# The second pass of a token mix: the 64 leftover rows ahead of the first pair of row tiles

## The chip, the cores and the metric

The kernel runs on one core of one Trainium2 chip. Its time is device microseconds of one execution; the figure for the kernel before is the median of three runs. The profile is of one execution, and its times are counted from the span's start.

## The reference

Two stages follow each other. The first is a long convolution of x (8 batches, 5696 steps, 128 channels) with h along the steps, by an FFT. The second takes its result as x:

```python
theta = x @ w_theta
zr, zi = x * np.cos(theta), x * np.sin(theta)
y = np.einsum('ts,bsd->btd', w_tok_r, zr) + np.einsum('ts,bsd->btd', w_tok_i, zi)
u = x + y
out = u + np.maximum(u @ w_ch, 0.0)
```

The token mix, two 5696 x 5696 matrices against 5696 x 1024 values, is most of the matmul work, and the only part that the change touches.

## The kernel before

**The mix in two passes.** The 5696 steps are two halves of 2816 and 64 leftover ones. The contraction over s runs in two passes p, one for each half of s; the leftover s (`zl`) are added in the second pass. The output rows are 22 tiles of 128 in each half and 64 leftover rows. One step of the loop is a pair tt: tile tt of the first half together with tile 22 + tt of the second, for both halves of the batch, four sums of 128 x 512. Pass 0 leaves its sums in `cp_hbm`, pass 1 reads them as addends (`addend`), adds its own and hands each finished 128 x 512 tile to an output stage (`u_stage`: a transpose on TensorE, a copy on ScalarE, a product with `w_ch`, the maximum and sum on VectorE, a store).

**Stretches.** Each pair runs over 11 b tiles j (a b tile holds 128 contraction rows: real and imaginary parts of 64 steps, 4 blocks of 512 columns), in stretches of 3, 3, 3 and 2. `prepare(i)` makes the weights of stretch i: W is loaded as it lies in memory by GpSimd's queue into a ring of six slots (`load_w`, L504), and `w_t` (L709) transposes it on VectorE, one instruction of 128 x 384 words for each of the four blocks of W.

**Seven products or eight.** Most pairs use Strassen's scheme: seven products per j and r (L1079) instead of eight, into seven accumulators M1 to M7 in the order M3, M4, M5, M2, M1, M7, M6. It needs sums of W (`w_sum`, L718) and sums of b (`sum_ops`, L650: three into new blocks of the b tile, M3, M4 and M1, and two in place, over M6 and M7). A few pairs (`plain`) take the eight products of the plain scheme (L1000), which needs b as it was loaded: in pass 1 that is pair 0, so that the b sums can be made while it runs. The leftover rows (`tt is None`, L943 to L983) are 64 rows: 4 products per j and r (L963, L965) of 64 columns of weights, which still stream 512 columns of b. They take W from the matrices' last 64 rows, in loads of half the size.

**The start of pass 1.** `pairs` (L450) sets the order: in pass 1 pair 0, then the leftover, then pairs 1 to 21. `start_pass` (L834) issues, on ScalarE's DMA queue, the loads of the 11 b tiles of the second half (two of 512 KB each, L634), which wait until pass 0 has read the tiles; and on SyncE the two loads of `zl`, whose sum is made on VectorE (L842). While pair 0's stretches run, the first two b sums of each tile are issued (L1058); in the leftover, the other three (L971). The leftover uses W sums (`sa`, L864) with M2, M3, M4 and M5, and the accumulators of M1 and M7.

**The order of the instructions.** Each engine works through its own list. A scheduler orders them, but for VectorE between (1, 0, 0) and (1, 1, 0), i.e. from pass 1's pair 0 to its pair 1, where the order is as written (`manual_schedule`, L911). At the end of a pair that is followed by another pair (`woven`), the transposes for the next pair are put between the evacuations of the accumulators; ahead of the leftover they are made before the last stretch's matmuls. The output stages of a pair wait in a list (`spread`) and are issued one per stretch by `aside` (L935): the first half after one product, the second after another; in the leftover around its matmuls (L950, L968). DMAs on the hardware queues (SyncE's and ScalarE's) share eight semaphores, and each waits for the landing of the one before it on its own.

Of the kernel before, what the change touches and what calls it, by code (L numbers as in the profile page):

```python
# [22 lines left out]
def kernel(  # L23
# [423 lines left out]
                    nc.sync.dma_start(z_hbm[r, p_, j, q_, i], z[rows])  # L447

    CHUNKS = [(j0, min(CJ, NJ - j0)) for j0 in range(0, NJ, CJ)]
    pairs = (list(range(21)) + [None, 21], [0, None] + list(range(1, 22)))  # L450
    chunks = [(p, tt, c) for p in range(2) for tt in pairs[p] for c in range(len(CHUNKS))]
    ring = {"n": 0, "read": set(), "wl": 0, "upto": 0}
    loaded = {}
# [194 lines left out]
    def sum_ops(bt):  # L648
        b11, b12, b21, b22 = (bt[q] for q in (M2, M6, M7, M5))
        return [lambda f=f, x=x: f(*x) for f, x in (  # L650
            (nc.vector.tensor_sub, (bt[M3], b12, b22)), (nc.vector.tensor_sub, (bt[M4], b21, b11)),
            (nc.vector.tensor_add, (bt[M1], b11, b22)), (nc.vector.tensor_add, (b12, b11, b12)),
            (nc.vector.tensor_add, (b21, b21, b22)))]
# [53 lines left out]
    def w_t(wb, j0, nj, ng=4, pool=None):  # L707
        wt = (pool or tp).tile([P, TJ, P, 2], BF16, tag="ws" if pool else "wt", name="wt")
        nc.vector.transpose(  # L709
            wt.rearrange("p j t r -> p (j t r)").bitcast(F32).rearrange(  # L710
                "p (j g t) -> p g j t", j=TJ, g=4)[:, :ng, :nj],
            wb[:, :ng, j0 * 64:(j0 + nj) * 64].bitcast(F32).rearrange(
                "p g (j s) -> p g j s", j=nj))
        return wt

    def w_sum(x0, x1, op, nj, m=P):
        out_ = sp.tile([P, TJ, P, 2], BF16, tag="ws")
        nc.vector.tensor_tensor(out_[:, :nj, :m], x0[:, :nj, :m], x1[:, :nj, :m], op=op)  # L718
        return out_
# [88 lines left out]
    def addend(p, k, ti, h, m=P):  # L808

        tag = f"c{k}"  # L810
        if p == 1:
            tag = ("c0", "c1", "c2", "c3", "red", "mag")[tags["n"] % 6]
            tags["n"] += 1
        c = cp.tile([P, 512], F32, tag=tag, name=f"c{k}")
        if p == 0 and ti in (22, 23):
            yT = cp.tile([P, 4, P], BF16, tag=f"yy{k}", name=f"yy{k}")
            nc.sync.dma_start(yT, yt_hbm[:, 4 * h:4 * h + 4, ti * P:ti * P + P])
            return c, yT
        if p == 0:
            yy = cp.tile([P, 512], BF16, tag=f"yy{k}", name=f"yy{k}")  # L820
            nc.sync.dma_start(yy[:m], half(y2_hbm, ti, h)[:m])
            return c, yy
        nc.sync.dma_start(c[:m], half(cp_hbm, ti, h)[:m])
        return c, c
# [26 lines left out]
    def prepare(i, at_once=True):  # L851
        if i >= len(stretches):
            return None
        k, p, tt, j0, s0, nj = stretches[i]
        pump()

        def read():
            if s0 + nj == CHUNKS[chunks[k][2]][1]:
                ring["read"].add(k)
                pump()  # L860
        if tt is None:
            a1, a2 = (w_t(loaded[k][n], s0, nj, ng=2) for n in range(2))
            read()
            return a1, a2, w_sum(a1, a2, add, nj, m=64)  # L864
        w11, w12, w21, w22 = (loaded[k][n] for n in range(4))
        if plain(p, tt):
            a = {}

            def some(n):
                if n in (0, 1):  # L870
                    a[n] = w_t((w11, w12)[n], s0, nj)
                elif n in (4, 5):
                    a[n - 2] = w_t((w21, w22)[n - 4], s0, nj, pool=sp)
            if not at_once and p:
                return a, some
            for n in range(6):
                some(n)
            read()
            return a if at_once else (a, lambda n: None)
        a = {}  # L880

        def step(n):

            if n == 0:
                a[M3] = w_t(w11, s0, nj)
            elif n == 1:
                a[M4] = w_t(w22, s0, nj)
            elif n == 2:
                a["12"] = w_t(w12, s0, nj)
                a[M5] = w_sum(a[M3], a["12"], add, nj)  # L890
            elif n == 3:
                a["21"] = w_t(w21, s0, nj)
                a[M2] = w_sum(a["21"], a[M4], add, nj)
            elif n == 4:
                a[M1] = w_sum(a[M3], a[M4], add, nj)
            elif n == 5:
                a[M7] = w_sum(a["12"], a[M4], ALU.subtract, nj)
            else:
                a[M6] = w_sum(a["21"], a[M3], ALU.subtract, nj)
        if at_once:  # L900
            for n in range(7):
                step(n)
            read()
            return a
        return a, step
# [1 line left out]
    nxt, second, st = None, None, {}  # L907
    ordered = ExitStack()
    for i, (k, p, tt, j0, s0, nj) in enumerate(stretches):
        if (p, tt, j0 + s0) in ((0, 0, 0), (1, 0, 0)):  # L910
            ordered.enter_context(tc.manual_schedule(engines={mybir.EngineType.DVE}))  # L911
        elif (p, tt, j0 + s0) in ((0, 2, 6), (1, 1, 0)):
            ordered.close()
# [18 lines left out]
        a, nxt = nxt, None if i == 1 else prepare(i + 1, not woven)  # L932
        if woven:
            nxt, step = nxt
        def aside(first_of, second_of):  # L935
            nonlocal second
            if first_of and spread and (p == 1 or (tt > 0 and not end_of_pair)):
                where_bg["tags"] = ("c2", "c3") if j0 + s0 == TJ else ("red", "mag")
                _, first, second = spread.pop(0)
                with tc.issue_after(sides["late"].ins) if p == 0 and tt == 1 else ExitStack():  # L940
                    first()
                    if len(spread) > 1:
                        spread[1][0]()  # L943
            if second_of and second is not None:
                second()
                second = None

        if tt is None:
            if p:
                aside(True, False)  # L950
            if first_of_pair:
                ps = [mps.tile([P, 512], F32, tag=f"m{q}", name=f"m{q}") for q in ((M1, M7) if p else (M3, M4))]
                cs = [addend(p, h, NT - 1, h, m=64) for h in range(2)]
            a1, a2, sa = a
            terms = ((sa, M2, a2, M4), (a1, M3, sa, M5))
            for j in range(nj):
                jj = j0 + s0 + j
                for r in range(2):
                    b = [x[:, r, :] for x in bts[jj]]
                    st_ = jj == 0 and r == 0  # L960
                    sp_ = jj == NJ - 1 and r == 1 and zl is None
                    for h, (x0, q0, x1, q1) in enumerate(terms):
                        nc.tensor.matmul(ps[h][:64], x0[:, j, :64, r], b[q0],  # L963
                                         start=st_, stop=False)
                        nc.tensor.matmul(ps[h][:64], x1[:, j, :64, r], b[q1],  # L965
                                         start=False, stop=sp_)
            if p:
                aside(False, True)  # L968
            if p == 1:
                for j in range(nj):  # L970
                    for op in sum_ops(bts[j0 + s0 + j])[2:]:  # L971
                        op()
            if end_of_pair:
                if zl is not None:
                    wl = wl_room()
                    nc.sync.dma_start(wl[:, :64], wl_hbm[:, NT - 1, :64])
                    for h in range(2):
                        nc.tensor.matmul(ps[h][:64], wl[:, :64], zl[h], start=False, stop=True)
                for h in range(2):
                    c, c0 = cs[h]  # L980
                    nc.vector.tensor_add(c[:64], c0[:64], ps[h][:64])
                    finish(p, NT - 1, h, c, m=64)
            continue  # L983
        classic = plain(p, tt)
        if first_of_pair and i:
            ms = [mps.tile([P, 512], F32, tag=f"m{q}", name=f"m{q}") for q in (range(7) if not classic else (M3, M4, M5, M2) if p else (M2, M6, M1, M7))]
        if first_of_pair:
            where = ((tt, 1), (22 + tt, 0), (tt, 0), (22 + tt, 1))
            if zl is not None:
# [3 lines left out]
        if j0 + s0 == (3 if classic else 2) * TJ:  # L993
            cs = (sides["cs"] if p == 0 and tt == 0 else
                  [addend(p, n, t, h) for n, (t, h) in enumerate(where)])

        def product(a, jj, j, n, hs):
            for r in range(2):
# [30 lines left out]
        if classic:  # L1029
# [24 lines left out]
            for j in range(nj):  # L1054
                if p == 0:
                    done["used"] = tt * (j0 + s0 + nj)
                else:
                    for op in sum_ops(bts[j0 + s0 + j])[:2]:  # L1058
                        op()
        else:  # L1060
            left = {}
# [80 lines left out]
```

## Time and profile before

| | |
|---|---|
| median of three runs | 2114.66 us (2113.42 to 2116.9) |
| the profiled execution | 2114.66 us, span 2112.9 us |
| TensorE (PE) busy | 2000.1 us, 95% of the span |
| VectorE (DVE) busy | 1593.8 us, 75% |
| mean of one 128 x 512 x 128 matmul (L1079), pipelined | 380 ns |
| one b sum, 128 x 1024 (L650) | 649 to 685 ns |
| DMA share of 16 engines, 1260 to 1314 us | full |

The busy time of a matmul is from its start to its modelled end, and the next starts before that; so starts are compared, not busy times. "Idle before, releaser" behind a row of the timeline says how long the engine did nothing ahead of it and what ended that. The chain of waits goes back from the last instruction to what released it, step by step. The granted clock is the share of its full clock that TensorE had.

### The profile page before, as it was taken

To read this page: it belongs to the slowest core of one execution; us is meant where nothing else is said; L and a number is where in the kernel's file an instruction comes from. 1 tells how busy PE (TensorE), PEld (TensorE's weight loads), DVE (VectorE), ACT (ScalarE), POOL (GpSimd) and SP (SyncE) were. 2 spreads that over 40 slices of the span, in tenths; PEclk is the share of its full clock that TensorE was granted. 3 is DMA by queue.
4 is the path that set the end of the run, shared out by engine and by line. 5 is a ranking of instruction groups with operands and counts; after the bars stand their busy time and mean duration, and the time that the engine had idled before them with its cause. 6 is when DMAs were issued, how large, how long until landed. Compare 5 with 4: busy or idle time off the path is not lost.

```text
span 2112.9 us, 41491 instructions
## 1 busy us (share of the span) xinstructions
PE 2000.1 (95%) x15765; PEld 1115.9 (53%) x15765; DVE 1593.8 (75%) x2884; ACT 674.1 (32%) x997; POOL 906.6 (43%) x1662
## 2 busy tenths in 40 slices
PE   4788889878999999999999999999999999999998
PEld 3787888754444444444444444444444444444444
DVE  7767767776878888888886756877777777776867
ACT  5877878874332333232310000111111111111111
POOL 5301010237444636354556544445454444545450
PEclk8698889999999999999999999999999999999999
DMA  7357474999989989898999879768788887879793
GB/s 144 96 130 168 114 183 108 237 251 242 179 152 179 178 172 168 170 177 173 176 163 156 141 145 293 127 113 153 135 145 143 138 150 129 155 128 155 126 155 89
DMA packets 408264, 334.95 MB, mean 159 GB/s; under 512 B 85927, under 2 KB 358439, under 8 KB 407079
## 3 DMA queue, kind: packets, MB, share of 16 engines
q0 software_dynamic: 225952, 156.72, 52.4%
q1 hardware_dynamic: 176128, 164.05, 27.1%
q10 hardware_dynamic: 5984, 11.54, 1.6%
q8 instruction: 123, 2.02, 0.4%
q14 instruction: 77, 0.63, 0.1%
HBM read 377.11 MB, written 92.49 MB: 222 GB/s over the span
## 4 chain that ended last, share of the span: by engine, by line
PE 67%; DVE 3%; DMA 1%; issue 1%; POOL 0%; ACT 0%; DVEq 0%
PE m L1079 61%; PE m L1000 2%; DVE b L650 1%; PE v L796 1%; PE utp L789 1%; PE m L1083 1%; DVE c L1086 1%; DVE wt L709 1%; PE m L963 0%; PE m L965 0%; PE tpz L737 0%; PE theta_ps L391 0%; POOL ring L504 0%; DMA ring<-in_moe_w_tok_r_dram 0%; DMA wl<-in_moe_w_tok_i_dram 0%
## 5 line engine op out<-in xcount | busy, mean ns | idle before, releaser
L504 POOL DMA_DIRECT2D ring<-in_moe_w_tok_i_dram x720 | 387.9, 546 | 659.6 <-DVE wt L709 587.7
L709 DVE STREAM_TRANSPOSE wt<-ring 128x384 f32<-128x384 f32 (+2 forms) x720 | 358.6, 522 | 121.7 <-PE m L1079 70.6
L504 POOL DMA_DIRECT2D ring<-in_moe_w_tok_r_dram x720 | 386.4, 546 | 148.6 <-DVE wt L709 88.3
L1079 PE MATMUL m<-b,wt 128*128 128x512 bf16 x1640 | 389.2, 380 | 2.0 <-DVE wt L709 1.7
L1079 PEld LDWEIGHTS <-wt 128*128 128x128 bf16 x1804 | 176.5, 98 | 218.8 <-DVE wt L709 6.5
L1086 DVE TENSOR_TENSOR c<-c,m 128x512 f32<-128x512 f32 x412 | 264.7, 667 | 0.4 <-PE m L1079 0.4
L791 ACT ACTIVATE ring<-utp 128x512 bf16<-128x512 bf16 (+1 forms) x86 | 50.9, 592 | 586.7 <-PE utp L789 586.7
L323 PE MATMUL ps<-r_u,u_t 128*128 128x128 f16 x1024 | 130.8, 227 | 7.0 <-DVE u_t L307 6.3
L324 PE MATMUL ps<-r_v,v_t 128*128 128x128 f16 x1024 | 129.9, 227 | 0.0
L786 ACT ACTIVATE ub<-c 128x512 bf16<-128x512 f32 (+1 forms) x90 | 56.3, 628 | 213.2 <-DMA ring<-in_moe_w_tok_r_dram 120.9
L1000 PE MATMUL m<-b,wt 128*128 128x512 bf16 x480 | 112.5, 385 | 7.5 <-DMA b<-z_hbm 3.9
L129 POOL DMA_DIRECT2D x<-in_x_dram x64 | 33.9, 535 | 193.6 <-PE ps L193 181.1
L323 PEld LDWEIGHTS <-u_t 128*128 128x128 f16 x1024 | 105.7, 103 | 8.1 <-DVE u_t L307 8.1
L324 PEld LDWEIGHTS <-v_t 128*128 128x128 f16 x1024 | 104.8, 102 | 3.0 <-DVE v_t L307 1.3
L305 ACT ACTIVATE xs<-ps 128x1024 f16<-128x1024 f32 x96 | 95.3, 1017 | 13.2 <-DVE v_t L307 7.9
L307 DVE TENSOR_TENSOR u_t<-xs,hs 128x1024 f16<-128x1024 f16 x96 | 69.8, 727 | 33.4 <-ACT xs L305 23.6
L193 PE MATMUL ps<-f_t,x 89*128 89x180 f16 x512 | 82.0, 315 | 8.7 <-ACT xs L305 6.7
L1000 PEld LDWEIGHTS <-wt 128*128 128x128 bf16 x528 | 51.2, 99 | 68.9 <-issue 8.1
L211 PEld LDWEIGHTS <-w_t 64*128 64x128 f16 x3240 | 61.0, 102 | 36.5 <-issue 23.4
L193 PEld LDWEIGHTS <-x 89*128 89x128 f16 x512 | 73.4, 233 | 11.0 <-issue 10.1
L393 ACT ACTIVATE red<-theta_ps,magic 128x512 f32<-128x512 f32 (+1 forms) x46 | 31.6, 687 | 134.6 <-PE theta_ps L391 107.8
L739 ACT ACTIVATE ring<-tpz 128x512 bf16<-128x512 bf16 (+1 forms) x46 | 27.5, 597 | 131.7 <-PE tpz L737 111.0
(2912 smaller groups left out, 3883.3 us busy)
## 6 DMA issues: line engine op xcount, KB each, us to landing
ring<-in_moe_w_tok_r_dram POOLq DMA_DIRECT2D x352, 96.0 KB, 4.5
ring<-in_moe_w_tok_i_dram POOLq DMA_DIRECT2D x352, 96.0 KB, 4.8
ring<-in_moe_w_tok_r_dram POOLq DMA_DIRECT2D x352, 80.0 KB, 4.4
ring<-in_moe_w_tok_i_dram POOLq DMA_DIRECT2D x352, 80.0 KB, 3.9
hs<-hf_hbm SPq DMA_DIRECT2D x192, 128.0 KB, 3.3
cp_hbm<-c SPq DMA_DIRECT2D x88, 256.0 KB, 2.2
c<-cp_hbm SPq DMA_DIRECT2D x88, 256.0 KB, 4.5
out_dram<-c SPq DMA_DIRECT2D x88, 256.0 KB, 4.2
```

The source lines that it names most:

```text
L193: nc.tensor.matmul(ps[:, i // 2, (i % 2) * 2 * K1:(i % 2 + 1) * 2 * K1], lhs(q + i), f1_t[:NB], start=True, stop=True)
L211: nc.tensor.matmul(ps[:, e, j * HD:(j + 1) * HD], w_t2[rows, c0 + j, N2 * (1 - ri):N2 * (3 - ri)], a_st["a"][rows, ri * K1 + c0 + j, :], s ...
L305: nc.scalar.activation(xs[:, :, :, :ck], ps, AF.Copy)
L307: nc.vector.tensor_tensor(uv[r][:, :, :, c0:c0 + ck], xs[:, :, :, :ck], hv[:, r:r + 1, :, :ck].to_broadcast([P, 2, HD, ck]), op=mult)
L323: nc.tensor.matmul(o, u_t[:, at:at + P], r_u, start=True, stop=False)
L324: nc.tensor.matmul(o, v_t[:, at:at + P], r_v, start=False, stop=True)
L504: nc.gpsimd.dma_start(wb[32 * i:32 * i + 32, :ng, :nj * 64], bass.AP(tensor=a.tensor, offset=a.offset + row0 * S + p * H + i * QR + j0 * 6 ...
L709: nc.vector.transpose(wt.rearrange("p j t r -> p (j t r)").bitcast(F32).rearrange("p (j g t) -> p g j t", j=TJ, g=4)[:, :ng, :nj], wb[:, : ...
L786: nc.scalar.activation(ub[:m].rearrange("p b d -> p (b d)"), c[:m], AF.Copy)
L1000: nc.tensor.matmul(ms[n // 2 * 2 + h], a[n][:, j, :, r], bts_of[p][jj][n % 2 * 2 + h][:, r, :], start=(n % 2 == 0 and jj == 0 and r == 0), ...
L1079: nc.tensor.matmul(ms[q], a[q][:, j, :, r], bts[jj][q][:, r, :], start=(jj == 0 and r == 0), stop=(jj == NJ - 1 and r == 1 and q not in left))
L1086: nc.vector.tensor_tensor(c, z, ms[q], op=op)
```

## The change

In pass 1 the order becomes leftover, pair 0, pairs 1 to 21. With it:

- the leftover uses no W sums: its two sums are a1 x M2 + a2 x M7 and a1 x M6 + a2 x M5, with b as loaded, in the accumulators of M2 and M6; pair 0 takes those of M7, M5, M1 and M3 (it had M3, M4, M5, M2);
- three b sums of each tile (M3, M4, M1) are issued in the leftover, the two in place in pair 0;
- no output stage is issued in the leftover; pair 0's four come in pair 1, and the leftover's two in pair 0;
- pair 0's transposes aren't woven into the last stretch of pass 0 any more (the stretch before the leftover makes its transposes at once);
- VectorE's written order begins with the leftover.

```diff
-    pairs = (list(range(21)) + [None, 21], [0, None] + list(range(1, 22)))
+    pairs = (list(range(21)) + [None, 21], [None] + list(range(22)))
...
-            return a1, a2, w_sum(a1, a2, add, nj, m=64)
+            return a1, a2, None if p else w_sum(a1, a2, add, nj, m=64)
...
         if plain(p, tt):
-            a = {}
-
-            def some(n):
-                if n in (0, 1):
-                    a[n] = w_t((w11, w12)[n], s0, nj)
-                elif n in (4, 5):
-                    a[n - 2] = w_t((w21, w22)[n - 4], s0, nj, pool=sp)
-            if not at_once and p:
-                return a, some
-            for n in range(6):
-                some(n)
+            a = [w_t(w11, s0, nj), w_t(w12, s0, nj), w_t(w21, s0, nj, pool=sp), w_t(w22, s0, nj, pool=sp)]
             read()
             return a if at_once else (a, lambda n: None)
...
-        if (p, tt, j0 + s0) in ((0, 0, 0), (1, 0, 0)):
+        if (p, tt, j0 + s0) in ((0, 0, 0), (1, None, 0)):
             ordered.enter_context(tc.manual_schedule(engines={mybir.EngineType.DVE}))
...
         if tt is None:
-            if p:
-                aside(True, False)
             if first_of_pair:
-                ps = [mps.tile([P, 512], F32, tag=f"m{q}", name=f"m{q}") for q in ((M1, M7) if p else (M3, M4))]
+                ps = [mps.tile([P, 512], F32, tag=f"m{q}", name=f"m{q}") for q in ((M2, M6) if p else (M3, M4))]
...
-            terms = ((sa, M2, a2, M4), (a1, M3, sa, M5))
+            terms = (((a1, M2, a2, M7), (a1, M6, a2, M5)) if sa is None else
+                     ((sa, M2, a2, M4), (a1, M3, sa, M5)))
...
-            if p:
-                aside(False, True)
             if p == 1:
                 for j in range(nj):
-                    for op in sum_ops(bts[j0 + s0 + j])[2:]:
+                    for op in sum_ops(bts[j0 + s0 + j])[:3]:
                         op()
...
-            ms = [... for q in (range(7) if not classic else (M3, M4, M5, M2) if p else (M2, M6, M1, M7))]
+            ms = [... for q in (range(7) if not classic else (M7, M5, M1, M3) if p else (M2, M6, M1, M7))]
...
                 else:
-                    for op in sum_ops(bts[j0 + s0 + j])[:2]:
+                    for op in sum_ops(bts[j0 + s0 + j])[3:]:
                         op()
```

As built, VectorE has four instructions less (the leftover's W sums of pass 1), and PE, ScalarE, GpSimd and SyncE have as many as before in another order. On PE the leftover's first stretch is ordered by accumulator: twelve matmuls into M2, then twelve into M6. At the end of pair 0 the list of PE is: pair 0's last matmuls, the transposes and then the product of an output stage, then pair 1's first matmuls. On VectorE: pair 0's four evacuations, then three transposes for pair 1. On SyncE the leftover's two addends are loaded behind `zl` and the stores of pass 0's last pair, and two of pair 0's four addends far ahead of them, during pass 0. On GpSimd the leftover's four W loads stand ahead of pair 0's eight.

More of the change, by code (lines that the diff above doesn't have):

```diff
@@ L934 @@
             nxt, step = nxt
[L935 to L946, printed above, removed]
         if tt is None:
-            if p:
-                aside(True, False)
             if first_of_pair:
-                ps = [mps.tile([P, 512], F32, tag=f"m{q}", name=f"m{q}") for q in ((M1, M7) if p else (M3, M4))]
+                ps = [mps.tile([P, 512], F32, tag=f"m{q}", name=f"m{q}") for q in ((M2, M6) if p else (M3, M4))]
                 cs = [addend(p, h, NT - 1, h, m=64) for h in range(2)]
             a1, a2, sa = a
-            terms = ((sa, M2, a2, M4), (a1, M3, sa, M5))
+            terms = (((a1, M2, a2, M7), (a1, M6, a2, M5)) if sa is None else
+                     ((sa, M2, a2, M4), (a1, M3, sa, M5)))
             for j in range(nj):
@@ L985 @@
         if first_of_pair and i:
-            ms = [mps.tile([P, 512], F32, tag=f"m{q}", name=f"m{q}") for q in (range(7) if not classic else (M3, M4, M5, M2) if p else (M2, M6, M1, M7))]
+            ms = [mps.tile([P, 512], F32, tag=f"m{q}", name=f"m{q}") for q in (range(7) if not classic else (M7, M5, M1, M3) if p else (M2, M6, M1, M7))]
         if first_of_pair:
@@ L995, with aside @@
                   [addend(p, n, t, h) for n, (t, h) in enumerate(where)])
+        def aside(first_of, second_of):
+            nonlocal second
+            if first_of and spread and (p == 1 or (tt > 0 and not end_of_pair)):
+                where_bg["tags"] = ("c2", "c3") if j0 + s0 == TJ else ("red", "mag")
+                _, first, second = spread.pop(0)
+                with tc.issue_after(sides["late"].ins) if p == 0 and tt == 1 else ExitStack():
+                    first()
+                    if len(spread) > 1:
+                        spread[1][0]()
+            if second_of and second is not None:
+                second()
+                second = None
         def product(a, jj, j, n, hs):
```

## The prediction

> **What bounds the kernel now.** I read the page's busy row and chain first, for the whole span.
>
> ```profile
> PE 2000.1 (95%) x15765; PEld 1115.9 (53%) x15765; DVE 1593.8 (75%) x2884; ACT 674.1 (32%) x997; POOL 906.6 (43%) x1662
> ...
> PE 67%; DVE 3%; DMA 1%; issue 1%; POOL 0%; ACT 0%; DVEq 0%
> ```
>
> TensorE (PE) sets the end; only a few per cent of the chain are waits. The change touches the start of the second pass alone, and leaves the number of matmuls as it is. So the question is how many microseconds PE loses there, before and after. The timeline of PE gives the stage's ends:
>
> ```profile
> 1283.08 1.03 PE L1000 MATMUL m<-ring,wt 128*128 128x512 bf16 x4
> ...
> 1346.04 0.62 PE L978 MATMUL m<-zl,ring 128*64 128x512 bf16 x2
> 1348.40 1.03 PE L1079 MATMUL m<-ring,wt 128*128 128x512 bf16 x2 [1.75 <-DVE wt L709]
> ...
> 1386.18 0.59 PE L1079 MATMUL m<-ring,wt 128*128 128x512 bf16 x2
> ```
>
> Pair 0 starts at 1283.08, the leftover ends at 1346.66, pair 1 starts at 1348.40, pair 2 at 1386.18: 103.1 us. Matmuls of 512 columns start 0.2158 us apart (pair 2's next stretch of 6 in 1.295 us). Pair 0 has 180, the leftover 90, pair 1 158: 428 x 0.2158 = 92.4. A full output stage costs PE 0.45 (pair 2 takes 1422.07 - 1386.18 = 35.89, less 158 x 0.2158, over four), a 64-row one about 0.4: four and two give 2.6. Pure work: **95.0 us; lost now: 8.1 us.** Where, the chain of waits says:
>
> ```profile
> 1335.70 5.41 DVE b L650 x9
> ...
> 1342.96 4.89 DVE b L650 x8
> 1347.86 0.50 DVE wt L709
> 1348.40 5.76 PE m L1079 x18
> ```
>
> VectorE (DVE) is late: nine sums of the leftover's stretch stand ahead of the transposes that PE waits for. Behind the 1.75 us of idle the clock is at half for one stretch of 3.4 us from 1348.5 (granted clock 0.96 over 1348 to 1386, 1.00 around it). Why DVE is late is in its own timeline, and in the DMA view of 1257 to 1316:
>
> ```profile
> 1291.15 0.42 DVE L842 TENSOR_TENSOR zl<-zl,zl 128x512 bf16<-128x512 bf16 x1 [4.47 <-DMA zl<-zl_hbm]
> ...
> 1303.34 0.58 DVE L709 STREAM_TRANSPOSE wt<-ring 128x384 f32<-128x384 f32 x1 [5.37 <-DMA ring<-in_moe_w_tok_r_dram]
> 1309.41 0.58 DVE L709 STREAM_TRANSPOSE wt<-ring 128x384 f32<-128x384 f32 x1 [5.50 <-DMA ring<-in_moe_w_tok_i_dram]
> ```
> ```profile
> q10 hardware_dynamic: 5984, 11.54, 55.6%
> q0 software_dynamic: 6204, 3.82, 43.7%
> q1 hardware_dynamic: 1510, 2.47, 12.8%
> ```
>
> The 22 half tiles of b (11.54 MB), the W loads and the small transfers fill all 16 DMA engines for 59 us; DVE idles 10.9 us for W. This case's b is just in time: b10's first half, issued at 1302.52, lands at 1313.82; pair 0 needs it at about 1315.
>
> **The change, part by part.**
>
> *The leftover first, pair 0 second.* PE's counts stay: 90 and 180. But PE eats the b tiles twice as fast: 24 matmuls per stretch of three tiles (5.2 us) instead of 48 (10.4). Without any wait the leftover would run from 1283.1 to 1302.5, and would need b10 from 1300.4, 15 us sooner than now. This is the term that decides.
>
> When does the last b half land? The three queues' shares give 32.8, 25.8 and 7.6 us of full DMA time, 66.2 in 59, so I scale by 0.89: 2.54 us per MB of b, 6.0 of W, 2.74 of the small ones. b needs 29.3 us whatever happens. Of W, the leftover's loads (48 and 40 KB each instead of 96 and 80) now come ahead of pair 0's, and six ring slots gate the rest: the first pair's end 0.6 MB, the leftover 0.70, two loads of pair 0 0.77, two more (freed by the transposes of the leftover's second stretch, near 1289) 0.77, a part of the next two 0.16: 3.0 MB, 18.1 us, against 23.0 now. Small transfers 6. Sum 53.4: b lands by 1310.4; I take **1310**. Bounds: at the bare 2.54 us per MB, if W yields wholly, PE isn't held by b (1257 + 29.3 = 1286); with nothing gained, 1316, the present end of the full stretch. The middle is nearest to the row because W keeps a load in flight most of the time.
>
> With b10 at 1310, eight matmuls and the two of zl follow (2.2): the leftover ends at 1312.2 instead of 1302.5. **Loss 9.7 us.** It covers DVE's own chain: zl lands near 1288 to 1291 (its second half is issued when b4's second half lands, 1285.16 now, on the same DMA semaphore), the second stretch's transposes are queued behind that add, then three times nine sums (5.5 each by the rows above) with two half transposes (0.63 a pair) between, then pair 0's transposes: 1289 + 0.6 + 16.5 + 1.3 = 1307.4 to 1310, sooner than 1312.2. So DVE is hidden, but only by some 2 to 5 us; if b came early, DVE would be the bound.
>
> *Four sums of W less (L718), half transposes sooner.* 3 x 0.36 + 0.29 = 1.4 us of DVE, not on the path. Nothing. The leftover's loads and transposes stand in the same number; pair 0's second half of W comes later but pair 0 needs it 20 us after its start.
>
> *M2 and M6 for the leftover.* M6 is the accumulator that pass 0 empties last (1286.03 to 1286.68). The changed program puts twelve matmuls into M2 first, from M2's own evacuation at about 1283.4, so M6 is asked for at 1286.0: 0.3 us, within the 9.7.
>
> *b sums split 3 and 2 instead of 2 and 3.* 55 sums of 0.61 as before. The two in place now stand in pair 0 (10.4 us of PE for 3.7 of DVE) instead of three in the leftover (5.2 for 5.5): that removes the present wait for late sums, the **8.1 us** above with its half clock.
>
> *Pair 0 directly ahead of pair 1.* Pair 1's first transposes were made ahead of the leftover's end; now they stand on DVE behind pair 0's last two evacuations. After PE's last matmul: about 0.2 to the result, 1.28 for two evacuations (1321.92, L1041), 0.5 for a transpose, 0.1: 2.1 us. On PE an output stage is queued there too (its four transposes, then a wait for ScalarE's copy, 0.60, then four matmuls); it lies within the gap and fills 0.45 of it. **Net 1.7.** Behind it are pair 1's matmuls alone. The idle is like the 1.75 us that brought the half clock: 3.4 us at half, **1.7** more. Bounds 0 and 3.4 (a second such stretch in the leftover's stalls).
>
> The Trainium skill, TensorE: Matmul & The Clock Gate, "Why this matters for your kernels", asks for no idle gap over some 3 us; by it this gap would leave the clock alone and the result would be 1.7 lower. This trace has the half clock behind a gap of 1.75.
>
> *Output stages moved from the leftover to pair 1, ScalarE's and SyncE's orders with them.* Same count; two leftover ones go to pair 0, four to pair 1, whose reserve is that of pair 2 (35.89 with four). On SyncE zl keeps its place; two addends of pair 0 go far ahead, two of the leftover behind the first two stores. Nothing.
>
> **Sum.** 95.0 + 9.7 + 1.7 + 1.7 = 108.1 against 103.1: +5.0. The profiled execution took 2114.66 (span 2112.9 and 1.8 around it), which is also the median of the runs. **2114.66 + 5.0 = 2119.7 us.**
>
> **Rivals.**
>
> *b keeps its pace.* ACT's and POOL's queues both always have work, and halved W loads only follow each other sooner; b10 lands at 1316. For it: b's halves land 2.4 us apart whatever W load is beside them. Against it: the ring has no free slot around 1285. Leftover end 1318.2, loss 15.7, a second half clock 1.7: 95.0 + 15.7 + 3.4 + 1.7 = 115.8, +12.7: 2127.4. DMA: Bandwidth & Descriptors of the Trainium skill, "Queues, rings and completion order", has the engines take turns between queues packet by packet, which speaks for this one: b's share then does not depend on how large a W load is. No run here shows it yet.
>
> *A tie.* b lands at 1306 to 1307, when DVE is ready too: loss 6, gap 1.7, half clock 1.7: 104.4, +1.3: 2116.
>
> *Faster: DVE's late sums were the only cost.* With W out of the way (the ring is empty from about 1285 to 1289) b10 lands before 1303.5; then DVE's chain alone, with zl at 1287, starts pair 0 at 1306, loss 3.5, gap 1.7, no half clock: 100.2, -2.9: 2111.8; with zl before PE's need as well, down to 2109. It decides from b10 at 1303.5; for it the 10.9 us of DVE idle on W that go, against it the 53 us of DMA work.
>
> That the change does nothing is excluded: the built program's order shows the leftover's 90 matmuls ahead of pair 0's.
>
> **How the numbers follow.** Forecast (2118 to 2123) 0.43; b keeps its pace 0.15; tie 0.22; faster 0.20, of which 0.13 ends over 0.2% below. 0.2% (4.2 us) is about what a measurement of this kernel tells from no change; the forecast lies just over it. Slower 0.43 + 0.15 = 0.58; same 0.22 + 0.07 = 0.29; faster 0.13. The range takes in the rivals' centres: 2111 to 2128.
>
> **What would show it.** Right: the leftover starts at 1283, its fourth stretch waits on "DMA b" and it ends near 1312; the sums' share of the chain falls; a gap of 2 us ahead of pair 1 that ends with a transpose, with a granted clock under 1.00 behind it; pair 2 starts near 1391. Wrong: no wait on b (then DVE's sums must be the releaser and the time is below before's), or waits on W ahead of pair 0, which I cost at nothing; or b10 landing past 1313.

## The result and the profile after

| | before | after |
|---|---|---|
| median of four runs each | 2114.28 us (2113.42 to 2116.9) | **2124.3 us** (2121.02 to 2128.6) |
| the profiled execution | 2114.66 us, span 2112.9 | 2124.24 us, span 2122.5 |
| pass 1's first matmul to pair 2's first | 103.1 us | 112.2 us |

The change makes the kernel slower: 1.0046 times the time before, 95% interval [1.0026, 1.0067]. The forecast was 2119.7, with 2111 to 2128 as its range. The two profiled executions differ by 9.6 us, and the stage between pass 1's start and pair 2 alone by 9.1. The rest of the program is as long as it was within 0.5 us, so the loss is in the stage that the prediction looked at. (In the changed kernel pair 0's products are L989, the leftover's L941 and L943, those of the pairs behind L1068; numbers below L860 are as before.)

The page's busy row and the shares of the chain show little, as TensorE still sets the end with the same work. Of the chain, DVE has 1% where it had 3, and DMA 2% where it had 1, and that is the story in short:

```profile
PE 1998.5 (94%) x15765; PEld 1115.6 (53%) x15765; DVE 1596.1 (75%) x2880; ACT 676.1 (32%) x997; POOL 908.0 (43%) x1662
...
PE 67%; DMA 2%; DVE 1%; issue 1%; POOL 0%; ACT 0%; DVEq 0%; ACTq 0%
```

TensorE's timeline of the changed kernel, with only the rows that have an idle time ahead of them or begin a part (start, length, group, idle time and what ended it):

```profile
1283.46 0.38 PE L941 MATMUL m<-ring,wt 128*64 128x512 bf16 x1
...
1291.46 0.41 PE L941 MATMUL m<-b,wt 128*64 128x512 bf16 x1 [2.66 <-DVE wt L709]
...
1297.39 0.41 PE L941 MATMUL m<-b,wt 128*64 128x512 bf16 x1 [0.52 <-DVE wt L709]
...
1302.54 0.38 PE L943 MATMUL m<-b,wt 128*64 128x512 bf16 x1 [1.25 <-DMA b<-z_hbm]
...
1305.62 0.38 PE L941 MATMUL m<-b,wt 128*64 128x512 bf16 x1 [1.41 <-DMA b<-z_hbm]
1308.90 0.58 PE L943 MATMUL m<-b,wt 128*64 128x512 bf16 x1 [2.90 <-DMA b<-z_hbm]
...
1314.30 0.58 PE L943 MATMUL m<-b,wt 128*64 128x512 bf16 x1 [1.83 <-DMA b<-z_hbm]
...
1317.99 1.04 PE L989 MATMUL m<-ring,wt 128*128 128x512 bf16 x4
...
1359.54 0.40 PE L796 MATMUL v<-w_ch_sb,ring 128*128 128x128 bf16 x4 [0.75 <-ACT ring L791]
1360.22 0.61 PE L1068 MATMUL m<-ring,wt 128*128 128x512 bf16 x2 [0.28 <-DVE wt L709]
...
1395.67 0.59 PE L1068 MATMUL m<-ring,wt 128*128 128x512 bf16 x2
```

The leftover starts at 1283.46 and pair 0 at 1317.99: 34.5 us for 90 matmuls that need 19.4. The matmuls' starts, taken one by one, divide the 15.1 us: 3.5 are two waits on VectorE's transposes, 8.3 are four waits on b, and the rest, some 3.3, is mostly 16 matmuls that start 0.38 to 0.43 us apart instead of 0.2158. Those have half the clock, as the table by stretches says (its columns: stretch, length, busy time of PE, PEld, DVE, ACT and POOL with their instructions, granted clock, DMA share, GB/s):

```profile
1303.00:1309.00 6.00, 1.69 (x8) 0.73 (x7) 6.00 (x12) 0.00 (x0) 3.64 (x7) 0.87 1.10 331
1309.00:1314.30 5.30, 3.47 (x9) 1.24 (x8) 3.49 (x7) 0.00 (x0) 0.70 (x2) 0.50 1.03 197
1314.30:1318.00 3.70, 3.70 (x10) 1.35 (x9) 2.02 (x4) 0.00 (x0) 0.00 (x0) 0.54 0.05 8
```

The half clock lasts from 1307.4 to 1317.7, three of the trace's records of the granted clock, 3.4 us each. Behind the gap ahead of pair 1 (pair 0's matmuls end at 1358.4, pair 1 begins at 1360.22) there is none. What the chain of waits follows back through the leftover is three loads of b. The first was issued behind a load that waited until pass 0 had read its tile, the second when the first, on the same semaphore, had landed, and the third directly behind a load that waited for the second in the same way:

```profile
1276.88 15.76 DMA b<-z_hbm
1292.65 9.85 DMA b<-z_hbm
...
1302.98 11.28 DMA b<-z_hbm
1314.30 0.58 PE m L943
```

The last half of b10 lands at 1314.26, 30.8 us behind the leftover's start.

### The profile page after: what moved, and what is told of

Read it like the earlier page. It is cut to its first block, busy times and chain, and to the rows that moved or that the text cites. A ratio compares the mean times of both kernels' runs of the same rounds, so it can differ in the third digit from the quotient of the medians.

```text
span 2122.5 us, 41480 instructions
## 1 busy us (share of the span) xinstructions
PE 1998.5 (94%) x15765; PEld 1115.6 (53%) x15765; DVE 1596.1 (75%) x2880; ACT 676.1 (32%) x997; POOL 908.0 (43%) x1662
## 4 chain that ended last, share of the span: by engine, by line
PE 67%; DMA 2%; DVE 1%; issue 1%; POOL 0%; ACT 0%; DVEq 0%; ACTq 0%
PE m L1068 60%; PE m L989 2%; DMA b<-z_hbm 2%; PE v L796 1%; PE utp L789 1%; PE m L1072 1%; DVE c L1075 1%; PE m L943 1%; PE m L941 1%; PE theta_ps L391 0%; POOL ring L504 0%; PE tpz L737 0%; DVE wt L709 0%; DMA wl<-in_moe_w_tok_i_dram 0%; DMA ring<-in_moe_w_tok_r_dram 0%
## 5 line engine op out<-in xcount | busy, mean ns | idle before, releaser
L1068 PE MATMUL m<-b,wt 128*128 128x512 bf16 x1640 | 388.3, 379 | 2.0 <-DVE wt L709 1.7
L1068 PEld LDWEIGHTS <-wt 128*128 128x128 bf16 x1804 | 176.1, 98 | 215.5 <-DVE wt L709 4.4
L989 PE MATMUL m<-b,wt 128*128 128x512 bf16 x480 | 112.4, 384 | 7.1 <-DMA b<-z_hbm 4.1
L307 DVE TENSOR_TENSOR u_t<-xs,hs 128x1024 f16<-128x1024 f16 x96 | 70.2, 731 | 30.5 <-ACT xs L305 20.4
L989 PEld LDWEIGHTS <-wt 128*128 128x128 bf16 x528 | 50.8, 99 | 69.1 <-issue 9.7
L193 PEld LDWEIGHTS <-x 89*128 89x128 f16 x512 | 73.1, 234 | 11.2 <-issue 10.7
L393 ACT ACTIVATE red<-theta_ps,magic 128x512 f32<-128x512 f32 (+1 forms) x46 | 31.6, 687 | 134.9 <-PE theta_ps L391 108.5
L798 DVE SCALAR_TENSOR_TENSOR c<-v,c 128x512 f32<-128x512 f32 (+1 forms) x90 | 61.1, 681 | 11.5 <-PE v L796 11.5
```

Of the source, the lines that this page charges most:

```text
L193: nc.tensor.matmul(ps[:, i // 2, (i % 2) * 2 * K1:(i % 2 + 1) * 2 * K1], lhs(q + i), f1_t[:NB], start=True, stop=True)
L307: nc.vector.tensor_tensor(uv[r][:, :, :, c0:c0 + ck], xs[:, :, :, :ck], hv[:, r:r + 1, :, :ck].to_broadcast([P, 2, HD, ck]), op=mult)
L798: nc.vector.scalar_tensor_tensor(c[:m], v[:m], 0.0, c[:m], op0=ALU.max, op1=ALU.add)
L989: nc.tensor.matmul(ms[n // 2 * 2 + h], a[n][:, j, :, r], bts_of[p][jj][n % 2 * 2 + h][:, r, :], start=(n % 2 == 0 and jj == 0 and r == 0), ...
L1068: nc.tensor.matmul(ms[q], a[q][:, j, :, r], bts[jj][q][:, r, :], start=(jj == 0 and r == 0), stop=(jj == NJ - 1 and r == 1 and q not in left))
```

## The experiments

**Theory A**, the prediction's: the leftover eats b at twice the pace and waits for its last tile, which shares the DMA engines with W. **Theory B**: VectorE's chain (the sum of zl, nine b sums per stretch, then pair 0's transposes) sets the end of the leftover. **Theory C**: b is late because each load waits on its semaphore for an earlier landing, whatever the traffic.

Pass 1 starts anywhere between 1281 and 1291 us in the profiles of these runs, whatever the kernel, because pass 0 and the convolution vary. So stages are compared from pass 1's first matmul on, in one profile of each run, beside the timed ratios. The kernel before, run again beside each group, had medians of 2115.4, 2117.0 and 2115.3 us; the ratios are against these runs. All the numbers by stage:

| run | b10 lands after the start | pair 0 (or leftover) begins after | to pair 2's start | time, median | ratio to before |
|---|---|---|---|---|---|
| before | 30.7 (its first half) | 39.2 (leftover) | 103.1 | 2114.28 | 1 |
| after | 30.8 | 34.5 | 112.2 | 2124.3 | 1.0046 [1.0026, 1.0067] |
| E1 without four W loads | 23.4 | 25.7 | 103.1 | 2117.11 | 0.9998 [0.9986, 1.0011] |
| E2 third W load on held | 23.9 | 27.9 | 112.7 | 2122.63 | 1.0037 [1.0024, 1.0051] |
| E3 zl's sum later | 32.3 | 34.6 | 112.0 | 2123.08 | 1.0037 [1.0023, 1.0052] |
| E4 pair 0 first, no stages in the leftover | 34.8 | 45.3 (leftover) | 100.9 | 2205.68 | 1.042 [1.039, 1.0449] |
| E5 pair 0 first, stages back | 34.4 | 44.0 (leftover) | 102.8 | 2115.46 | 1.0000 [0.9986, 1.0014] |
| E6 before, sums put off | 34.7 | 40.7 (leftover) | 108.5 | 2121.86 | 1.0025 [1.0012, 1.0039] |
| E7 fifth and sixth W load held | 27.3 | 31.0 | 108.5 | 2120.59 | 1.0015 [1.0003, 1.0027] |
| E8 before, sums put off otherwise | 34.3 | 40.2 (leftover) | 101.5 | 2116.62 | 0.9999 [0.9986, 1.0013] |
| E9 E5, sums in W's waits | 35.5 | 41.0 (leftover) | 99.8 | 2113.17 | 0.9988 [0.9976, 0.9999] |

### E1: four of pair 0's W loads left out

```diff
-            loaded[k][n] = load_w(a, row0, p, *CHUNKS[c], ng=ng)
+            loaded[k][n] = load_w(a, row0, p, *CHUNKS[c], ng=ng, skip=p == 1 and tt == 0 and n // 2 != c)
...
-        for i in range(4):
+        for i in range(0 if skip else 4):
```

> The changed kernel without four of the eight W loads of pair 0 in the second pass (the third to sixth; its transposes read what the ring still holds, so pair 0's products have wrong W values). The place, size and number of everything else stay. Theory A (the last b tile shares the DMA engines with pair 0's W loads): these four loads are issued from 1291.7 to 1310 and hold about 1.4 MB; without them b10 lands 4 to 5 us earlier, near 1309, the leftover ends near 1313 and the time falls by 4 to 6 us, to about 2119. Theory B (VectorE's chain of sums sets the end of the leftover): the last sums are late by 2 to 3 us less than b10, so at most 2 us fall, and the releaser ahead of pair 0 becomes VectorE's wt. Theory C (b10 waits for the semaphore that b8's second half holds, not for bandwidth): b8 lands when it lands, b10 is issued within 1 us of 1302.6 and the time stays within 2 us of 2124.

The fall is larger than theory A asked for: b10 lands 7.4 us sooner after the start, no half clock is granted in the stage, and the stage is back at 103.1 us. The DMA view of the changed kernel from the leftover's start to b10's landing (queue, packets, MB, share of the 16 engines' time; q10 is b's queue, q0 W's, q1 the small transfers'):

```profile
q10 hardware_dynamic: 3047, 5.86, 53.6%
q0 software_dynamic: 2657, 1.68, 36.3%
q1 hardware_dynamic: 1247, 2.03, 19.9%
```

and that of E1 for the same part:

```profile
q10 hardware_dynamic: 2978, 5.72, 69.3%
q1 hardware_dynamic: 1248, 2.03, 24.7%
q0 software_dynamic: 344, 0.23, 6.3%
```

b's 5.8 MB cost the engines nearly the same packet time in both: 53.6% of 30.9 us is 16.6, and 69.3% of 23.4 is 16.2. (Packets overlap: the three shares add up to 110% in the changed kernel and to 100% in E1.) What went is W's time, 11.2 us down to 1.5. So b's pace is what W leaves it. That is theory A. Theory C falls as a cause: b10's last half is still issued directly behind a load that waits on its semaphore for an earlier landing, but that landing itself comes sooner when W is away (b10's last half is issued 15.4 us after the start instead of 19.5).

### E2: W held from pair 0's third load on

```diff
+        if hold:
+            nc.gpsimd.tensor_copy(wb[:, 0, 0:1], bts_of[1][NJ - 1][M5][:, 0, 0:1])
```

with hold for the third and fourth load of pair 0 in pass 1, on GpSimd's queue, so that all later W loads stand behind it.

> The changed kernel with the third and fourth W loads of pair 0 held back until the last half of b10 has landed (a one-column copy on GpSimd from b10 into each of the two ring slots); the later W loads queue behind them. All data are loaded. Theory A: b10 lands near 1308, 5 to 6 us earlier; pair 0's first two loads are there already, its third and fourth land 5 to 6 us behind b10, near 1314, and are wanted when pair 0's first stretch needs its second half of W, 5 us behind its start: 3 to 5 us less than the changed kernel, about 2120. If W then comes too late, pair 0 waits on transposes (wt, behind ring) and the gain is lost: 2124 or more. Theory C: b10 is not sooner and W is later: 2126 or more.

b10 lands 6.9 us sooner after the start, as theory A had it, and pair 0 begins 6.6 us sooner. Then the gain is given back: the stage takes 112.7 us, and the time, 2122.63, lies between the two that were named. The place is not the one that I had named either: it is not TensorE's products that wait for the late transposes, but the leftover's results. VectorE's timeline of E2 (L711 is the transpose here, L652 a b sum, L959 the leftover's results), and TensorE's row behind them:

```profile
1315.14 0.58 DVE L711 STREAM_TRANSPOSE wt<-ring 128x384 f32<-128x384 f32 x1 [5.18 <-DMA ring<-in_moe_w_tok_r_dram]
1318.00 0.58 DVE L711 STREAM_TRANSPOSE wt<-ring 128x384 f32<-128x384 f32 x1 [2.28 <-DMA ring<-in_moe_w_tok_i_dram]
1318.50 3.66 DVE L652 TENSOR_TENSOR b<-b 128x1024 bf16<-128x1024 bf16 x6
1322.08 1.27 DVE L959 TENSOR_TENSOR c<-c,m 64x512 f32<-64x512 f32 x2
...
1323.47 0.39 PE L791 MATMUL utp<-ident_bf,ub 64*128 64x64 bf16 x4 [4.38 <-ACT ub L788]
```

VectorE waits 5.2 and 2.3 us for W with six sums and the results behind it in its list. The leftover's output stage, which TensorE has in the middle of pair 0, waits 4.4 us for them, two records of half clock follow, and pair 0 takes 47.3 us instead of 40.2.

### E3: the sum of zl behind the leftover's b sums

```diff
-            nc.vector.tensor_add(zl[2], zl[0], zl[1])
...
+                    nc.vector.tensor_add(zl[2], zl[0], zl[1])
```

> The changed kernel with VectorE's add of zl (which waits 4.9 us for its load, ahead of the second stretch's transposes) moved behind the b sums of a stretch. Theory A: the 2.66 us wait for wt at 1291 goes, but the leftover still ends when b10 lands: 0 to 1 us less, 2123 to 2124. Theory B: the chain on VectorE is what counts: 2.7 us or more fall, 2121.5 or less.

As theory A had it, and against B. VectorE now makes the sum of zl behind the leftover's last b sums. E3's waits of TensorE on b in this stage (its leftover's products are L940 and L942; us in all, times, longest):

```profile
PE m L942 <- DMA b<-z_hbm: 9.4, 4, 3.0
PE m L940 <- DMA b<-z_hbm: 1.4, 3, 0.8
```

The 3.2 us of waits on transposes are gone, and the waits on b have grown from 7.4 in the same view of the changed kernel (6.0 and 1.4) to 10.8. The stage is 112.0 us long. The time ratio is 0.0009 lower than the change's, within both intervals. A wait that goes ahead of a later deadline is worth nothing.

### E4 and E5: the order put back

E4 is the changed kernel with pair 0 first, the accumulators that go with that, three sums per tile in pair 0 and two in the leftover:

```diff
-    pairs = (list(range(21)) + [None, 21], [None] + list(range(22)))
+    pairs = (list(range(21)) + [None, 21], [0, None] + list(range(1, 22)))
```

> The changed kernel with the order alone put back: pair 0 first, the leftover second, with the accumulators that go with that, and three b sums per tile in pair 0, two in the leftover. What stays of the change: the leftover on unsummed b, no output stages inside it, pair 0's transposes at once. Theory A (order and the landing of b are the whole loss): b10 is needed near 1315 again and lands about then; VectorE has 6 sums instead of 9 per stretch of the leftover, so the lateness of 8 us of the kernel before shrinks: 2107 to 2113. Rival (the edits that stay cost the time: the lost overlap of output stages, transposes at once): 2118 or more.

Up to pair 2 the expectation holds: 100.9 us. Then the run loses over 90 us, for a reason that I had not seen. With pair 0 first, six finished tiles wait for their output stage from pair 1 on, because the changed leftover issues none; each pair issues four and adds four, so six stay, and the last two tiles never get theirs (two output tiles are left unwritten in this run). The addends rotate through six buffers, so each load waits for a stage that has just been issued. The group of VectorE's evacuations on E4's page shows it, with 56 us of waiting for addends, where the changed kernel has none:

```profile
L1075 DVE TENSOR_TENSOR c<-c,m 128x512 f32<-128x512 f32 x412 | 269.1, 676 | 57.1 <-DMA c<-cp_hbm 56.3
```

So E4's time says nothing of the order. E5 issues four output stages in the leftover again (`aside` around each stretch's matmuls, as the kernel before does).

> As the run with pair 0 first, but with the output stages inside the leftover again, so that the queue of finished tiles keeps its length: of the change there remain the unsummed b in the leftover, the split of the sums (three in pair 0, two in the leftover) and pair 0's transposes made at once. Theory A (the order is the loss, through the landing of b): the stage from the pass's start to pair 2 takes 101 to 104 us as in that run, against 103.1 before and 112.2 in the changed kernel, and the time is 2112 to 2115. Rival (the edits that stay carry a part of the loss): 2118 or more.

With 102.8 us and a ratio of 1.0000 the whole loss is undone by the order and the output stages that go with it; that the stages are not what counts up to pair 2 is seen from E4's 100.9 us without them. The edits that stay (b unsummed in the leftover, the split of the sums, pair 0's transposes at once) carry none of the loss that shows. What they do is move the wait: the 1.75 us ahead of pair 1 are 0.3 now, but in pair 0 the fourth stretch's transposes come late, because VectorE waits for W with nine sums still to do:

```profile
1309.59 0.58 DVE L709 STREAM_TRANSPOSE wt<-ring 128x384 f32<-128x384 f32 x1 [6.98 <-DMA ring<-in_moe_w_tok_i_dram]
1310.09 5.46 DVE L650 TENSOR_TENSOR b<-b 128x1024 bf16<-128x1024 bf16 x9
1315.47 1.42 DVE L709 STREAM_TRANSPOSE wt<-ring 128x256 f32<-128x256 f32 x4
```

TensorE waits 2.9 us for the last of these rows, with one record of half clock behind it.

### E6 and E8: the kernel before with its late sums put off

E6 is the kernel before, but each leftover stretch's nine sums are issued one stretch later, and the last stretch's in pair 1:

```diff
-                for j in range(nj):
-                    for op in sum_ops(bts[j0 + s0 + j])[2:]:
-                        op()
+                put_off.append([op for j in range(nj) for op in sum_ops(bts[j0 + s0 + j])[2:]])
+                if s0 + j0 and not end_of_pair:
+                    for op in put_off.pop(0):
+                        op()
+                elif end_of_pair:
+                    for op in put_off.pop(0):
+                        op()
```

> The kernel before, in its own order, with one edit on VectorE: the nine b sums of a leftover's stretch are put off by one stretch, so that pair 1's first transposes stand behind 9 sums less, and the last stretch's sums stand behind the transposes of pair 1's second stretch. If VectorE's late sums are the whole of the 8.1 us lost in this stage, the 1.75 us gap ahead of pair 1 and the half clock behind it go, and the waits of 0.2 to 0.5 us inside the leftover too: 4 to 7 us less, 2108 to 2111. Rival (the sums are wanted by pair 1 as early as the transposes are, so that the wait only moves into pair 1): 2113 to 2116.

Slower, and more than the rival had said: 108.5 us. TensorE's waits in E6 (L1087 is pair 1's product, L989 the leftover's results):

```profile
PE m L1087 <- DVE c L989: 4.7, 1, 4.7
PE m L1087 <- DVE wt L709: 2.0, 1, 2.0
```

The gap ahead of pair 1 stayed, since the put-off sums stood behind an output stage's last operation (L798), for which VectorE waited 1.5 and 4.45 us in the leftover. And the results stood behind nine sums, so that pair 1 waited 4.7 us for the accumulators, with one record of half clock behind it. E8 mends both: the sums ahead of that operation, and the last two stretches' sums behind the results.

> The kernel before, in its own order, with the leftover's b sums put off as in the run with the sums put off by one stretch, but so that they stand ahead of the output stage's last operation on VectorE (there VectorE waited 1.5 and 4.5 us for TensorE with the sums behind it), and the last two stretches' sums behind the leftover's results (there 5.5 us of sums stood ahead of them, and pair 1 waited 4.8 us for the accumulators). If VectorE's order is what the kernel before loses in this stage, from the pass's start to pair 2 it takes 97 to 99 us instead of 103.1 and the time falls by 4 to 6 us. Rival (sums put off at all come back as a wait in pair 1): 103 us or more, no gain.

101.5 us and no difference in time that the interval shows. The 4.7 us are gone, but 2.6 us of waiting for pair 1's second transposes have come, since the nine sums stand ahead of those now. The rival is nearer than the theory: in this list of VectorE's a sum that is put off comes back as another wait.

### E7: only the fifth and sixth W load held

As E2, with the hold on the first two loads of pair 0's second half.

> The changed kernel with the fifth and sixth W loads of pair 0 (the first of its second half) held behind b10's landing by one-column copies on GpSimd, the third and fourth left where they are. Theory A (each MB of W ahead of b10 costs b what it takes of the DMA engines): about 0.5 MB of W leaves the stretch ahead of b10, which lands 2 to 4 us earlier, near 1311; pair 0's second half of W is wanted 20 us behind its start, so nothing is late, unlike with the third and fourth held: 2119 to 2122. Rival (the two b halves that are left in flight then are limited by their own queue, W or not): b10 at 1314, 2124.

As theory A had it: W in flight ahead of b10 falls from 1.68 to 1.03 MB, b10 lands 27.3 us after the start instead of 30.8, nothing is late behind it, and the stage takes 108.5 us. The rival falls. TensorE does not wait for b10 itself any more: the leftover's last matmuls, at half clock from 1308.8 us on, are what ends it (the half clock lasts 6.8 us instead of 10.2).

### E9: E5 with the sums in VectorE's waits for W

```diff
+            if p == 1 and j0 + s0 == 2 * TJ:
+                for j in range(TJ, 2 * TJ):
+                    for op in sum_ops(bts_of[1][j])[:3]:
+                        op()
```

between the first two and the last two transposes of pair 0's third stretch, and not behind them.

> The kernel with the order put back (output stages in the leftover), with one edit on VectorE: the nine sums of pair 0's second stretch stand ahead of the second half of the third stretch's transposes, where VectorE waited 3.2 and 7.0 us for W loads, instead of behind it. There the fourth stretch's transposes came 3.1 us late and a half clock of 3.4 us followed. If that order is its only loss left, the 3.1 us and the half clock (1.7) go: 98 us from the pass's start to pair 2 instead of 102.8, and a time 4 to 5 us below that run, 0.2% below the kernel before. Rival (the transposes then wait for W or b instead): no gain.

The 2.9 us and their half clock are gone; TensorE's longest wait from 1275 to 1400 is 0.7 us:

```profile
PE m L996 <- DMA b<-z_hbm: 1.0, 2, 0.7
PE m L996 <- DVE c L1082: 0.6, 1, 0.6
PE m L1075 <- DVE wt L709: 0.3, 1, 0.3
PE m L1075 <- DVE c L977: 0.2, 1, 0.2
```

99.8 us, 3.0 less than E5 and not the 4.8 expected: b, 35.5 us after the start, is waited for now. Its ratio is the lowest of all, 0.9988 [0.9976, 0.9999] of the time before, a gain of 0.1% that the runs only just show. So a part of what the kernel before loses at this place, 3.3 of 8.1 us, could be had with pair 0 first; E5's edits and the order of VectorE's list, taken together, did it.

## Why the prediction was right, and where its size was off

In the prediction's own terms, from pass 1's start to pair 2's:

| | predicted | measured |
|---|---|---|
| leftover | 29.1 | 34.5 |
| pair 0 and pair 1, with their stages | 75.6 | 76.3 |
| gap ahead of pair 1, less the 0.45 of an output stage in it | 1.7 | 1.4 |
| half clock behind it | 1.7 | 0 |
| sum | 108.1 | 112.2 |

- **"Pure work"** was right to 0.7 us. Pair 1 with its four stages takes 35.9 us, as pair 2 does; the two 64-row stages cost pair 0 0.8 us each, where 0.4 was reckoned.
- **The leftover's loss** was named rightly, the fourth stretch's wait on b included, and E1, E5 and E7 show it. Its size was off by 5.4 us: "I take 1310" was 3.9 us too early, once the pass's later start is taken off, and the last ten matmuls, put at 2.2 us, took 3.7 at half clock. "Or b10 landing past 1313" stood among the prediction's own signs of being wrong, and it came true. The mis-sized term is W's traffic. Over 1257 to 1315 the changed kernel's queues show

```profile
q10 hardware_dynamic: 5984, 11.54, 57.2%
q0 software_dynamic: 5534, 3.40, 40.5%
q1 hardware_dynamic: 1312, 2.10, 11.0%
```

  Scaled to a full 100% as in the prediction, W took 21.6 us of the 58, where 18.1 were reckoned with, b 30.5 where it was 29.3, and the rest 5.9 where it was 6. W moved 3.4 MB and not 3.0, and at 6.4 us per MB and not 6.0: the loads of pair 0's second half, of which 0.16 MB had been reckoned with, were issued from 1303.5 on, and the later b10 was, the more of them went ahead of it.
- **"DVE is hidden, but only by some 2 to 5 us"**: right that it is hidden; the margin was larger, as b came later. Pair 0's transposes began at 1308.7, predicted 1307.4 to 1310, and were done at 1310.7, 7 us before pair 0 began, and then VectorE itself waited for b10. E3 shows that 2.7 us of its chain could go at no gain.
- **The gap ahead of pair 1** came nearly as worked out: 1.8 us with the output stage in it, where 2.1 were reckoned. **The half clock behind it** did not come, in this run nor in E1, E2, E3 and E7, which have much the same gap; it came inside the leftover, where the prediction had it as a bound. So the sum is nearer than its parts by luck: the term that did not come covers 1.7 of the 5.4 us by which the leftover was put too short.
- **The rivals.** "b keeps its pace" had b10 at 1316 and 2127.4 us. The result lies between it and the forecast, and nearer to it: 2124.3 us, with b10 at 1313.9 on the prediction's scale. b's pace does depend on W, since without the four W loads b's share rises from 54 to 69%, but the changed kernel moves nearly as much W as before, 3.4 MB against 3.8. The Trainium skill, DMA: Bandwidth & Descriptors, "Queues, rings and completion order", on which it drew, has the engines take turns packet by packet; the DMA view above agrees, with 2657 packets of W to 3047 of b, so that W takes nearly as many turns as b although it moves 29% of its bytes. "A tie" is what E1 made: there b10 lands 23.4 us after the start, which is 1306.5 on the prediction's scale, and the stage takes 103.1 where the rival had 104.4. So even a b that comes 7 us sooner would only have paid for the gap and not won. "Faster" asked for b10 by 1303.5, which not even E1 reaches.

## What to carry to other kernels

When a step that consumes loaded tiles faster is moved to the place where the tiles have only just been asked for, reckon the landing of the last tile from all the bytes that the DMA engines have to move until then, and let the transfers of other queues grow with the delay: a late tile lets more of the competing loads in. To hold the competing load back helps only if nothing else on an in-order engine stands behind the work that needs it (E2 against E7). And where one engine's written list is nearly full, each step that is put off has to be followed to whoever stands behind its new place; the place that paid was one where the engine waited for data anyway (E9).

## What the runs showed of the hardware that was not expected

- **The half clock does not follow from the length of one gap.** TensorE's single waits of 2.0 us (E6, ahead of pair 1) and 2.6 us (E8) brought none, one of 2.9 us (E5) and one of 1.75 us (before) brought one record of 3.4 us each. Four waits of 0.5 to 1.3 us ahead of the end of the leftover brought none in E1, and four of 0.5 to 1.5 us at the same place brought one in E2 (granted clock 0.54 from 1309.0 to 1312.7). In the changed kernel four waits of 1.25 to 2.9 us within 12 us, with one to eight matmuls between, brought three records in a row, and the third covers a stretch in which TensorE no longer waited. The Trainium skill, TensorE: Matmul & The Clock Gate, "Why this matters for your kernels", asks for no gap over some 3 us. The waits of 2.0 and 2.6 us in E6 and E8 agree with that; the kernel before, E5 and the broken-up waits do not, and for those the measurement decides: in the changed kernel broken-up waits, each under 3 us, cost some 3.3 us beyond their own length. What the records depend on is not settled by these runs.
- **A MB of W cost the engines more than twice a MB of b.** In packet time b cost 2.84 us per MB in the changed kernel (16.6 us for 5.86 MB) and 2.83 in E1 (16.2 for 5.72), with little W beside it; W cost 6.7 (11.2 for 1.68). Packet times overlap when queues share the engines, so with the shares scaled to 100% b's price in the changed kernel is 2.6.
